# A zeroing that waits for the first normalised tiles, and a weight load that changes queue

## The chip, the cores and the metric

The kernel runs on one core of a Trainium2 chip. The core has five engines with instruction queues of their own: TensorE (PE in the profile; its weight loads are listed as PEld), VectorE (DVE), ScalarE (ACT), GpSimd (POOL) and SyncE (SP), which here only issues DMA transfers. Any of the engines can issue transfers; the DMA engines behind them are shared. The metric is the device time of one execution in microseconds, as the median of several runs. The time before is 667.74 us, the median of three runs (665.72, 667.74 and 669.32).

## The reference

The input x has 2048 rows of 512. It is normalised by rows, and the result xn feeds two branches whose product is added to x:

```python
xn = _layernorm(x, axis=-1)
s = _A_ref(xn, A_wq, A_wk, A_wv, A_wo)   # attention: 32 heads of 16 for q, one shared k and v
g = _silu(_B_ref(xn, B_w1, B_w2))        # silu(xn @ w1) @ w2, F = 1792
return x + s * g
# in _A_ref:
scores = jnp.einsum("bhqd,bkd->bhqk", q, k) * (Dh ** -0.5)
p = _softmax(scores, axis=-1)
o = jnp.einsum("bhqk,bkd->bhqd", p, v)
```

With 32 heads, 2048 queries and 2048 keys there are 134 million exponentials, and the head dimension is only 16.

## The kernel before, in words

**Tiling.** The 2048 queries are cut into four chunks of 512 and the 32 heads into eight groups of four, which gives 32 groups (gi). For each group the keys go by in 16 tiles of 128. One score block has 128 keys by 512 queries of one head. TensorE computes the score blocks of four heads in four row strips of its array (`score`, L622). Keys are kept in two layouts, kTa and kTb (`kT_sb[0]` and `kT_sb[1]`). Even groups read kTa, odd ones kTb, whose rows are copied from kTa by DMA inside SBUF (`move_K`, L510: four transfers of 16 KB for each chunk of keys, on SyncE's queue).

**Exponentials.** Most blocks go to ScalarE, two at a time (`exp_A`, L653, 128 x 1024). The rest go to VectorE, which builds the bit pattern of an approximate exponential as int16 (`exp_D`, L691); GpSimd adds constants to it for two more terms (`shift`, L716). The product of the weights with v (L776) gathers in the bank psO.

**Masked q.** The tile `qm_sb` has four rows of blocks, one for each head of a group, zero everywhere except in the 32 partitions of its head. With it, a score block can also be computed by the whole array in column form (`col_fill`, which goes through the helper `columns`, L401). `mask_q` (L1324) fills the four rows by four DMA transfers of 32 KB from `qT_sb`, on SyncE's queue. Before that the tile has to be zeroed once: that is the memset at L389, on GpSimd. Each later refill of a row waits until the matmuls that read the row are done.

**The start.** Four tiles of x arrive; VectorE and ScalarE make their statistics, ScalarE takes the square root (L443), and VectorE normalises the four tiles (`normalise`, L450). TensorE transposes them (`first_T`, L477), ScalarE and VectorE copy the transposes out of PSUM in turn (L482, L484), then come the first keys and queries, and with them the first exponential. TensorE is kept busy until then by 13 warm-up matmuls on zeros (L408). The other twelve tiles of x are normalised beside the first exponentials; this is called the front in the code. When the last chunk of keys is there, `front_evac` calls `move_K` and then `late_loads`, which asks for wo (L395, on SyncE's queue) and w2 (L396, on ScalarE's queue). w1 was asked for earlier (L392, SyncE). The hidden layer (`h` jobs, w1) and its second product (`z` jobs, w2) fill TensorE between score blocks, through L401.

**The order.** A planner in Python (`Sched` and the loop at the end) lays out all instructions when the kernel is built. It models the time of every engine, t, and appends each operation to its engine's list. On the chip, each engine works its list off in order. An operation that reads or writes what another engine or a transfer still uses gets a semaphore wait, and the instructions behind it on the same engine wait too. The planner's times decide the order only; they do not delay anything on the chip.

Of the kernel before, what the change touches and what calls it, by code (L numbers as in the profile page):

```python
# [13 lines left out]
P = 128  # L14
# [21 lines left out]
class Sched:  # L36
# [107 lines left out]
    def op(self, eng, fn, reads=(), writes=(), lane=None, cost=None):  # L144
        who = lane or eng
        if lane:
            self.lanes[lane] = eng
        n = self.done.get(who, 0)
        self.done[who] = n + 1
        deps = self.deps(eng, reads, writes)  # L150
        self.at[(who, n)] = self.model(eng, lane, cost, max([self.at[d] for d in deps.items()], default=0.0))
        clk = self.clock.setdefault(eng, {})
        waits = []
        cand = [(f, m) for f, m in deps.items() if clk.get(f, -1) < m]
        for f, m in cand:
            implied = False
            for f2, m2 in cand:
                if (f2, m2) != (f, m) and self.snap[(f2, m2)].get(f, -1) >= m:
                    implied = True
            if not implied:  # L160
                waits.append((f, m))
        for f, m in cand:
            for g, k in self.snap[(f, m)].items():
                if clk.get(g, -1) < k:
                    clk[g] = k
            if clk.get(f, -1) < m:
                clk[f] = m
        for f, m in waits:
            self.flagged.setdefault(f, set()).add(m)
        self.snap[(who, n)] = dict(clk)  # L170
        self.queues.setdefault(eng, []).append((fn, waits, who, n))
        for r in reads:
            self.readers.setdefault(r, {})[who] = n
        for w in writes:
            self.last_w[w] = (who, n)
            self.readers[w] = {}
        return who, n
# [36 lines left out]
def bass_recurrent_scan__grouped_kv_mqa__dense_activation_silu__prompt_kernel(  # L214
# [69 lines left out]
        P=(0.25, 3.0, 0.65, 10, 1.2, 2.0, 0, 12, 0.2, 3, 3, 0.0, 0.35, 0.43, 0, 0.33, 0, 1, 9, 9),  # L284
# [10 lines left out]
        a=(0.3, 3.0, 0.65, 10, 1.2, 2.0, -4, 24, 0.2, 3, 3, 0.04, 9, 0.43, 0, 0.33, 0, 0, 9, 9),  # L295
# [5 lines left out]
    with ExitStack() as es:  # L301
        def sb(name, shape, dt=BF16):
            return es.enter_context(nc.sbuf_tensor(name, shape, dt))
# [11 lines left out]
        w2_sb = sb("w2_sb", [P, NFT, D])  # L315
# [11 lines left out]
        qm_sb = sb("qm_sb", [P, 4, NQ])  # L327
# [21 lines left out]
        op = K.op  # L349
# [5 lines left out]
           reads=["ident"], writes=["ident"])  # L355
# [19 lines left out]
        for j in range(NPH + 1):  # L375
# [10 lines left out]
        wkp4 = wkp_sb[:, :, :].rearrange("p c (r e) -> p c r e", e=32)  # L386
        op("gp", lambda e: e.tensor_copy(wkp4[:, :, :, 0:DH], wkn_sb[:, :, :].unsqueeze(2).to_broadcast([P, NDC, 4, DH])),
           reads=["wkn", "wkp"], writes=["wkp"])
        op("gp", lambda e: e.memset(qm_sb[:], 0.0), writes=[("qm", i) for i in range(4)], cost=1.8)  # L389

        def load_w1():
            op("sp", lambda e: e.dma_start(w1_sb[:], B_w1.rearrange("(dc p) f -> p dc f", p=P)), writes=["w1"], lane="lw1", cost=7.0)  # L392

        def late_loads():
            op("sp", lambda e: e.dma_start(wop_sb[:], A_wo.rearrange("(t p) n -> p t n", p=P)), writes=["wop"], lane="lwo", cost=4.0)  # L395
            op("a", lambda e: e.dma_start(w2_sb[:], B_w2.rearrange("(ft p) n -> p ft n", p=P)), writes=["w2"], lane="lw2", cost=9.0)  # L396

        def columns(e, bank, lhsT, rhs, start, stop):

# [13 lines left out]
        def tiles(c):  # L413
            return range(4 * c, 4 * c + 4)
# [34 lines left out]
        def normalise(t, eng):  # L449
            op(eng, lambda e: e.tensor_scalar(xn_sb[:, t % 8, :], x_sb[:, t, :], mv_sb[:, t, 0:1], rstd_sb[:, t:t + 1],  # L450
                                              op0=ALU.subtract, op1=ALU.mult),
               reads=[("x", t), ("mv", t), ("rstd", t // 4)], writes=[("xn", t % 8)], cost=0.41)
# [18 lines left out]
        def first_T(t, bank, key, eng):  # L471

            ps = bank.bitcast(BF16)[:, 0:NQ]

            def f(e):
                for dc in range(NDC):
                    r = e.transpose(ps[:, dc * P:(dc + 1) * P], xn_sb[:, t, dc * P:(dc + 1) * P], ident[:, :])  # L477
                return r
            op("pe", f, reads=[("xn", t), "ident"], writes=[key], cost=("full", [None] * 4, P))
            dst, src = xnT_sb[:, :, t * P:(t + 1) * P], ps.rearrange("p (dc q) -> p dc q", dc=NDC)  # L480
            if eng == "a":
                op("a", lambda e: e.activation(dst, src, ACT.Copy), reads=[key], writes=[("xnT", 0, t)])  # L482
            else:
                op("v", lambda e: e.tensor_copy(dst, src), reads=[key], writes=[("xnT", 0, t)])  # L484
# [71 lines left out]
        rstd_sqrt(0)  # L556
        for t in tiles(0):
            normalise(t, "v")
        first_T(0, psD[:, 0:NQ], "D", EV[0])
        first_T(1, psD[:, NQ:2 * NQ], "D1", EV[1])  # L560
        first_T(2, psO[:, :], "O", EV[2])
# [377 lines left out]
        def group_A():  # L939
            if ast["tile"] is not None:  # L940
                return ast["tile"][0]
            return next((gi for gi in range(NGRP) if left[gi] or halves.get(gi)), NGRP)
# [207 lines left out]
        qm = dict(of=-1)  # L1150
# [59 lines left out]
        def meets(t):  # L1210

            x = needed() + SLIP - t
            return 0 if x >= 0 else 1 + int(-x / 0.9175)

        def v_cand():

            tv = K.free["v"] - 0.084
            cand = [(max(tv, K.ready("v", tk["reads"], tk["writes"])), tk) for tk in tasks if all(n in tok for n in tk["need"])]
            d, blks = 1e9, dst["fifo"][:1]
            if blks and may_D(blks):  # L1220
                blk = blks[0]
                d = max(tv, K.ready("v", [blk["bank"]], [ph_key(0, slot_of[blk["idx"]], blk["pos"])]))
                two = dst["fifo"][:2]
                if len(two) == 2 and (two[0]["bank"], two[1]["bank"]) == ("D", "D1") and two[0]["idx"] == two[1]["idx"] and may_D(two):
                    d2 = max(tv, K.ready("v", ["D", "D1"], [ph_key(0, slot_of[b["idx"]], b["pos"]) for b in two]))
                    if d2 <= d + 0.1 and (JOINT or meets(d + 0.735) >= meets(d2 + 1.27)):
                        d, blks = d2, two
            return cand, d, blks

        def advance_v(t):  # L1230

            while True:
                cand, d, blks = v_cand()
                first = min([x for x, _ in cand] + [d])
                if first >= t:
                    return
                now = [(x, tk) for x, tk in cand if x <= first + 0.01]
                now.sort(key=lambda p: (p[1]["kind"] != "gn1", p[1]["kind"] in ("gn2", "gn3", "gn4", "add"), RANK.get(p[1]["kind"], 1), p[1].get("born", 0.0)))
                pick = now[0][1] if now else None
                if pick is not None and pick["kind"] == "st":  # L1240
                    soon = [(x, tk) for x, tk in cand if tk["kind"] in ("T", "K", "nm", "ag") and x < first + 0.35]
                    pick = min(soon, key=lambda p: p[0])[1] if soon else pick
                if pick is not None and d < first + pick["cost"] and first - pick.setdefault("born", first) < AGES.get(pick["kind"], AGE):
                    cost = 1.221 if len(blks) == 2 else 0.687
                    if meets(d + cost + 0.05) < meets(first + pick["cost"] + cost):
                        pick = None
                if pick is not None:
                    tasks.remove(pick)
                    pick["run"](pick)
                elif d < t:  # L1250
                    dst["fifo"] = dst["fifo"][len(blks):]
                    exp_D(blks)
                else:
                    return
# [151 lines left out]

        K.act_end = max(K.act_end, FIRST)
        K.free["a"] = max(K.free["a"], FIRST - 0.3)
        now, gp_end = 0.0, False
        while state["g"] < NGRP or front or jobs or jst["open"] or tasks:  # L1410
            (SLIP, ROUND, KEEP, HOLD, AGES["gn1"], AGE, F_BEHIND, ENDQ, PVWAIT, LEAD, AHEAD, MARGIN, XGAIN, AIM, TWIN,
             TGATE, FRESH, JOINT, CGAIN, CLEFT) = \
# [1 line left out]
            t = max(now, min(K.pe_next("col"), K.pe_next("full")))  # L1414
            if t > 2000.0:
                raise ValueError(f"the order does not end {state} {jobs[:3]} {jst} {tasks} {dst} {ast}")
            advance_v(t + 0.05)
            more = group_A() < NGRP
            if tanh_ready(K.act_end - TGATE if more else t):
                emit_tanh()  # L1420
            if not more and not gp_end and not dst["open"] and not dst["fifo"]:
                op("gp", lambda e: e.tensor_tensor(mhalf_sb[:, :], mhalf_sb[:, :], mhalf_sb[:, :], ALU.add),
                   reads=["mhalf"], writes=["mhalf"])
                gp_end = True
# [5 lines left out]
            if more:  # L1430
# [4 lines left out]
                if TWIN and K.pe_mode == "row" and not front and release() <= K.pe_next("row") + 0.12:  # L1435
                    slots, t = 0, K.pe_next("row")
# [41 lines left out]
            if TWIN and more and not blocked and did and not front and tanh_ready(K.act_end - TWIN):  # L1478
                emit_tanh()
                now = 0.0  # L1480
                continue
            if more and not blocked:
# [6 lines left out]
                now = 0.0  # L1489
            elif not did:  # L1490
                if dst["open"]:
                    fill_D(t, [0, 1, 2, 3])
                now = t + 0.05
            else:
                now = 0.0
# [38 lines left out]
        for k in (0, 1):  # L1534
# [13 lines left out]
           writes=[("out", t0), ("out", t0 + 1)], lane="st01a")  # L1548
# [40 lines left out]
```

## Time and profile before

| what | value |
|---|---|
| median of three runs | 667.74 us (665.72 to 669.32) |
| the profiled execution's own time | 666.98 us |
| its span, first to last instruction | 665.2 us |
| TensorE busy | 652.6 us (98%) |
| ScalarE busy | 652.6 us (98%), of which L653 630.9 us |
| VectorE busy | 597.5 us (90%) |
| GpSimd busy | 384.2 us (58%) |
| w2's load: KB, us from issue to landing | 1792, 9.5 |
| w1's load | 1792, 8.5 |

In the timeline a line has its start, its length, the engine, the line of the kernel, the operation, the tile written and the tile read, the shape and a count; in brackets stands how long the engine was idle before it and what ended that idle time. "xN" is N like instructions in a row, told as one. In a table of stages, each engine has its busy time and the number of instructions; then come the clock granted to TensorE, the mean busy share of the DMA engines, and GB/s. A busy TensorE is not a TensorE at full speed, since matmuls overlap and their ends are modelled.

### The profile page before, as it was taken

Reading aid. Unit: us, or ns where it says so; the run is one execution under the profiler, and the core shown is the slowest. Engines: PE = TensorE matmul, PEld = TensorE weight load, DVE = VectorE, ACT = ScalarE, POOL = GpSimd, SP = SyncE. Lnnn points to the kernel's source line nnn. Section 1 sums busy time; section 2 is a strip of 40 time slices with the busy share of each in tenths; the row PEclk is TensorE's granted clock in tenths of the full one; section 3 lists DMA queues with packets and bytes.
Section 4 is the critical chain, followed back from the end, with each engine's and each line's share of the span. In section 5 each row is a group of like instructions: output and inputs, shape, how many; then the busy total and the mean of one; then the engine's idle time right before and its main releaser. Section 6 shows DMA issues by size and latency. Waiting matters only on the chain.

```text
span 665.2 us, 18816 instructions
## 1 busy us (share of the span) xinstructions
PE 652.6 (98%) x8199; PEld 184.7 (28%) x8201; DVE 597.5 (90%) x1023; ACT 652.6 (98%) x754; POOL 384.2 (58%) x388
## 2 busy tenths in 40 slices
PE   8989999999999999999999999999999999999996
PEld 4422222222222222222222222222222222222221
DVE  7979899989888988989989889999999898898995
ACT  7979999999999999999999999999999999999997
POOL 4247455657655657565666656566665566675563
PEclk9979999999999999999999999999999999999999
DMA  5540000000000000100000000010000000000110
GB/s 168 160 153 2 1 8 6 2 9 2 6 1 10 2 25 18 39 4 2 9 2 6 6 3 2 8 33 26 25 4 5 1 8 16 1 2 2 33 34 33
DMA packets 15394, 14.61 MB, mean 22 GB/s; under 512 B 3536, under 2 KB 14800, under 8 KB 15312
## 3 DMA queue, kind: packets, MB, share of 16 engines
q1 hardware_dynamic: 12944, 11.05, 5.6%
q10 hardware_dynamic: 2368, 2.36, 1.2%
q8 instruction: 64, 1.05, 0.7%
q14 instruction: 18, 0.15, 0.1%
HBM read 8.95 MB, written 2.10 MB: 17 GB/s over the span
## 4 chain that ended last, share of the span: by engine, by line
ACT 77%; PE 17%; DVE 3%; DMA 1%; SPq 1%; issue 0%
ACT pa_sb L653 72%; PE psO L776 6%; PE psA L622 6%; ACT t_sb L1092 5%; PE psF L401 4%; DMA qm_sb<-qT_sb 1%; DVE stats_sb L417 1%; PE psD L461 0%; DMA x_sb<-in_A_x_dram 0%; DVE xn_sb L450 0%; SPq L510 0%; PE psD L492 0%; DVE kTa_sb L504 0%; PE psA L669 0%; DVE ph_sb L691 0%
## 5 line engine op out<-in xcount | busy, mean ns | idle before, releaser
L653 ACT ACTIVATE pa_sb<-psA 128x1024 bf16<-128x1024 f32 x662 | 630.9, 1220 | 5.0 <-PE psD L622 2.8
L716 POOL INT64_ADD ph_sb<-ph_sb x290 | 300.0, 1047 | 200.6 <-DVE ph_sb L691 200.4
L691 DVE TENSOR_SCALAR ph_sb<-psD 128x512 int16<-128x512 f32 (+1 forms) x520 | 348.0, 689 | 36.6 <-PE psD L622 31.7
L776 PE MATMUL psO<-ph_sb,vaug_sb 128*32 128x512 bf16 x1740 | 215.1, 384 | 0.0
L776 PE MATMUL psO<-pa_sb,vaug_sb 128*32 128x512 bf16 (+1 forms) x1332 | 201.3, 382 | 0.6 <-DVE onb_sb L888 0.6
L622 PE MATMUL psA<-qT_sb,kTa_sb 32*128 32x512 bf16 x684 | 132.7, 384 | 2.4 <-ACT pa_sb L653 1.2
L622 PE MATMUL psA<-qT_sb,kTb_sb 32*128 32x512 bf16 x632 | 123.1, 387 | 1.1 <-ACT pa_sb L653 0.6
L622 PE MATMUL psD<-qT_sb,kTb_sb 32*128 32x512 bf16 x325 | 114.7, 386 | 0.1
L716 POOL INT64_ADD x_sb<-x_sb x72 | 74.2, 1043 | 47.5 <-DVE x_sb L691 47.5
L691 DVE TENSOR_SCALAR x_sb<-psD 128x512 int16<-128x512 f32 x132 | 89.2, 684 | 12.6 <-PE psD L622 10.0
L622 PE MATMUL psD<-qT_sb,kTa_sb 32*128 32x512 bf16 x287 | 99.9, 384 | 0.0
L776 PE MATMUL psO<-x_sb,vaug_sb 128*32 128x512 bf16 x432 | 77.6, 383 | 0.0
L622 PEld LDWEIGHTS psA<-qT_sb,kTa_sb 32*128 32x128 bf16 x684 | 32.2, 91 | 143.1 <-ACT pa_sb L653 129.6
L401 PE MATMUL psF<-xnT_sb,w_sb 128*32 128x512 bf16 x896 | 69.8, 384 | 0.0
L401 PE MATMUL psF<-w_sb,u_sb 128*32 128x512 bf16 x896 | 69.5, 384 | 0.0
L622 PEld LDWEIGHTS psA<-qT_sb,kTb_sb 32*128 32x128 bf16 x632 | 29.8, 91 | 136.6 <-ACT pa_sb L653 121.4
L776 PEld LDWEIGHTS psO<-ph_sb,vaug_sb 128*32 128x32 bf16 x1740 | 53.2, 95 | 47.1 <-issue 30.4
L776 PEld LDWEIGHTS psO<-pa_sb,vaug_sb 128*32 128x32 bf16 x1332 | 48.9, 95 | 39.8 <-issue 29.4
L1092 ACT ACTIVATE t_sb<-psF 128x512 bf16<-128x512 f32 x72 | 57.8, 803 | 0.0
L1124 DVE SCALAR_TENSOR_TENSOR u_sb<-t_sb,psF 128x512 bf16<-128x512 bf16 x56 | 38.0, 679 | 4.9 <-ACT t_sb L1092 4.5
L691 DVE TENSOR_SCALAR ph_sb<-psF 128x512 int16<-128x512 f32 x52 | 35.4, 681 | 0.0
L622 PEld LDWEIGHTS psD<-qT_sb,kTb_sb 32*128 32x128 bf16 x325 | 27.5, 91 | 2.0 <-DVE ph_sb L691 1.1
(133 smaller groups left out, 368.1 us busy)
## 6 DMA issues: line engine op xcount, KB each, us to landing
x_sb<-in_A_x_dram SPq DMA_DIRECT2D x18, 128.0 KB, 2.2
qm_sb<-qT_sb SPq DMA_DIRECT2D x64, 32.0 KB, 1.8
w_sb<-in_B_w_dram SPq DMA_DIRECT2D x1, 1792.0 KB, 8.5
w_sb<-in_B_w_dram ACTq DMA_DIRECT2D x1, 1792.0 KB, 9.5
out_dram<-ob_sb SPq DMA_DIRECT2D x14, 128.0 KB, 1.7
x_sb<-in_A_x_dram SPq DMA_DIRECT2D x3, 512.0 KB, 6.6
wop_sb<-in_A_wo_dram SPq DMA_DIRECT2D x1, 512.0 KB, 7.9
wq_sb<-in_A_wq_dram SPq DMA_DIRECT2D x1, 384.0 KB, 6.1
```

The costliest lines, as they stand in the source:

```text
L401: r = e.matmul(bank[32 * i:32 * i + 32, :], lhsT=lhsT[:, 32 * i:32 * i + 32], rhs=rhs, start=start, stop=stop, tile_position=(0, 32 * i), ...
L417: op("v", lambda e: e.bn_stats(stats_sb[:, t, :], x_sb[:, t, :]), reads=[("x", t)], writes=[("st", t)], cost=0.687)
L622: return e.matmul(ap, lhsT=kT_sb[g % 2][32 * i:32 * i + 32, kt * P:(kt + 1) * P], rhs=qT_sb[32 * i:32 * i + 32, c % 2, g // 2, :], start=T ...
L653: d = op("a", lambda e: e.activation(pa_sb[:, sl, :], psA[k][:, :], ACT.Exp, scale=ESCALE), reads=["A%d" % k], writes=[("pa", sl)], cost=2 ...
L691: d = op("v", lambda e: e.tensor_scalar(ph_ap(0, sl, 512 * pos, 512 * pos + m), src, float(PH_ONE + PH_BIAS), 0.0, op0=ALU.add, op1=ALU.ma ...
L716: d = op("gp", lambda e, j=j: e.int64_add(ph_ap(j, sl, 0, 4 * NQ).bitcast(I64), ph_ap(0, sl, 0, 4 * NQ).bitcast(I64), PH_SHIFT[j] * 0x0001 ...
L776: r = e.matmul(psO[32 * i:32 * i + 32, cs], lhsT=vaug_sb[:, p["v"], p["kt"], :], rhs=p["ap"], start=s0, stop=s1, tile_position=(0, 32 * i) ...
L1092: op("a", lambda e: e.activation(t_sb[:, n % 2, :], bank_ap(b), ACT.Tanh, scale=0.5 if jb[0] == "h" else 0.25), reads=[b], writes=[("t", n ...
L1124: op("v", lambda e: e.scalar_tensor_tensor(out=dst, in0=t_sb[:, n % 2, :], scalar=1.0, in1=src, op0=ALU.add, op1=ALU.mult), reads=tk["read ...
```

## The change

Two things are edited. The memset that zeroes `qm_sb` is issued later in GpSimd's list's making, and it now reads ("xn", 3), the fourth normalised tile, so GpSimd waits for that tile before it zeroes. The load of w2 is taken out of `late_loads` and ScalarE's list. It becomes a function of its own, `load_w2`, on SyncE's list, which the planner's loop calls once, when its modelled time t first passes 60.

```diff
-        op("gp", lambda e: e.memset(qm_sb[:], 0.0), writes=[("qm", i) for i in range(4)], cost=1.8)
...
         def late_loads():
             op("sp", lambda e: e.dma_start(wop_sb[:], A_wo.rearrange("(t p) n -> p t n", p=P)), writes=["wop"], lane="lwo", cost=4.0)
-            op("a", lambda e: e.dma_start(w2_sb[:], B_w2.rearrange("(ft p) n -> p ft n", p=P)), writes=["w2"], lane="lw2", cost=9.0)
+
+        def load_w2():
+            op("sp", lambda e: e.dma_start(w2_sb[:], B_w2.rearrange("(ft p) n -> p ft n", p=P)), writes=["w2"], lane="lw2", cost=9.0)
...
         for t in tiles(0):
             normalise(t, "v")
+        op("gp", lambda e: e.memset(qm_sb[:], 0.0), reads=[("xn", 3)], writes=[("qm", i) for i in range(4)], cost=1.8)
...
-        now, gp_end = 0.0, False
+        now, gp_end, w2_asked = 0.0, False, False
...
             advance_v(t + 0.05)
+            if not w2_asked and t > 60:
+                load_w2()
+                w2_asked = True
```

## The prediction

> **What bounds the kernel now.** I read the page first: busy shares, the slices and the chain that ended last.
>
> ```profile
> span 665.2 us, 18816 instructions
> PE 652.6 (98%) x8199; PEld 184.7 (28%) x8201; DVE 597.5 (90%) x1023; ACT 652.6 (98%) x754; POOL 384.2 (58%) x388
> ACT 77%; PE 17%; DVE 3%; DMA 1%; SPq 1%; issue 0%
> ...
> L653 ACT ACTIVATE pa_sb<-psA 128x1024 bf16<-128x1024 f32 x662 | 630.9, 1220 | 5.0 <-PE psD L622 2.8
> ```
>
> ScalarE's exponentials (L653) are the bound. They run back to back from about 11 to 640 us, and of their 5.0 us of idle time the list of waits puts all in a few places. So only two things can shorten the run: an earlier first exponential, or less idle time between them. The timeline of ScalarE shows where that idle time is:
>
> ```profile
> 10.80 20.28 ACT L653 ACTIVATE pa_sb<-psA 128x1024 bf16<-128x1024 f32 x22 [0.59 <-PE psA L622]
> 30.89 0.39 ACTq L396 DMA_DIRECT2D w_sb<-in_B_w_dram  x1
> 30.92 8.41 ACT L653 ACTIVATE pa_sb<-psA 128x1024 bf16<-128x1024 f32 x9
> 40.39 1.02 ACT L653 ACTIVATE pa_sb<-psA 128x1024 bf16<-128x1024 f32 x1 [1.07 <-PE psD L622]
> 43.00 1.02 ACT L653 ACTIVATE pa_sb<-psA 128x1024 bf16<-128x1024 f32 x1 [1.58 <-PE psA L622]
> 44.94 1.02 ACT L653 ACTIVATE pa_sb<-psA 128x1024 bf16<-128x1024 f32 x1 [0.92 <-PE psD L622]
> 46.46 1.02 ACT L653 ACTIVATE pa_sb<-psA 128x1024 bf16<-128x1024 f32 x1 [0.50 <-PE psD L622]
> 47.82 7.44 ACT L653 ACTIVATE pa_sb<-psA 128x1024 bf16<-128x1024 f32 x8 [0.34 <-PE psD L622]
> ```
>
> Between 39.3 and 47.8 us ScalarE loses 1.07 + 1.58 + 0.92 + 0.50 + 0.34 = 4.41 us to late score matmuls. What made those late stands in TensorE's timeline and in the stages of that stretch (columns of the latter: PE, PEld, DVE, ACT, POOL busy, granted clock, DMA share, GB/s):
>
> ```profile
> 39.31 0.09 PEld L622 LDWEIGHTS psF<-qT_sb,kTb_sb 32*128 32x128 bf16 x1 [1.10 <-DMA kTb_sb<-kTa_sb]
> ...
> 41.80 0.11 PEld L401 LDWEIGHTS psD<-qm_sb,kTb_sb 128*32 128x32 bf16 x4 [1.42 <-DMA qm_sb<-qT_sb]
> ```
>
> ```profile
> 36.00:38.00 2.00, 2.00 (x24) 0.50 (x21) 1.83 (x3) 2.00 (x3) 0.70 (x2) 1.00 1.10 368
> 40.00:42.00 2.00, 0.88 (x15) 0.27 (x11) 1.74 (x3) 1.02 (x1) 0.00 (x0) 0.67 0.30 72
> 42.00:44.00 2.00, 2.00 (x18) 0.40 (x14) 0.85 (x2) 1.00 (x1) 0.74 (x1) 0.50 0.13 33
> 44.00:46.00 2.00, 2.00 (x18) 0.35 (x14) 1.03 (x2) 1.04 (x2) 1.31 (x2) 0.50 0.13 33
> ```
>
> The first two losses are TensorE waiting for copies inside SBUF (second key layout kTb, masked q). The last three are its clock, granted at 0.50 until past 46 us, with 512-column matmuls at 0.60 instead of 0.39 us. The DMA engines were full until 40 us, with w2's 1.8 MB, issued at 30.89 and 9.5 us in flight, as the largest part.
>
> The start is read on VectorE and GpSimd:
>
> ```profile
> 5.19 1.80 POOL L389 MEMSET qm_sb<- 128x2048 bf16 x1
> ...
> 6.04 1.10 DVE L450 TENSOR_SCALAR xn_sb<-x_sb,mv_sb,rstd_sb 128x512 bf16<-128x512 bf16 x1
> ...
> L450 DVE TENSOR_SCALAR xn_sb<-x_sb,mv_sb,rstd_sb x16: 395/407/1096, 6.0 to 27.6; 128x512 bf16<-128x512 bf16 x16
> ```
>
> The first normalise takes 1.10 us, the median of sixteen 0.41, and it ends 0.1 us after the memset does.
>
> **The change part by part.** Built, both programs have the same instructions in the same order on TensorE and VectorE. ScalarE loses one DMA issue, SyncE gains it between the eighth and ninth mask copy, and GpSimd's memset keeps its place and gains a wait. So nothing is reshuffled and the sum can be made by places.
>
> *Memset behind the fourth normalise.* The first normalise falls from 1.096 to 0.407, 0.69 us less, so all four end near 7.42 instead of 8.10. Two things may eat part of this: the warm-up matmuls, whose last starts at 6.27 and holds TensorE until about 6.6 (0.51 us less the usual overlap), and ScalarE's table load and its dummy exponential, which end at 7.31. With transposes every 0.32 us from 6.6, the second is done near 7.35 and ScalarE copies it out at 7.37 instead of 7.95: 0.58 less. VectorE's next input, the 512 KB of x issued at 2.65, lands 5.4 us later, at 8.05 by its issue's start or 8.56 by its end; the statistics that need it began at 8.69 and could begin at 8.1. In the second case they gain 0.1 only, and the key copy behind them (11.35) costs about 0.3 of the gain. Bounds 0.3 and 0.69; I take 0.5, nearer the earlier landing.
>
> The memset itself now runs from about 7.45 to 9.25. Behind it on GpSimd is only the inverse root at 11.5. Beside it lie two VectorE copies out of PSUM (L484, 0.41 each) and the statistics (0.68). Statistics beside the earlier memset of kTb (3.10 to 4.90) took 2.01 us for three, 0.67 each, so they are free. No row shows a bf16 copy out of PSUM beside a memset. Lower bound nothing, by L691, out of PSUM beside GpSimd all through (mean 0.689, and 0.68 with GpSimd idle); upper bound a block to the memset's end, as for the first normalise: the second copy then ends at 9.65 instead of 8.77, 0.9 us later than before. I take nothing, since L691 shares the PSUM source. On this the Trainium skill ("SBUF — State Buffer", Who interferes with whom; "VectorE: DVE Perf Modes", Mode 2×_2P) says that GpSimd and VectorE share one port pair under an exclusive lock, taken by VectorE's two-port modes, and that these need source and destination in SBUF. By that rule the copies are free as well; the 1.096 us row agrees with the lock, and no run here yet shows the copies.
>
> *w2 off ScalarE's queue.* The issue took 0.39 us, but exponentials come every 0.917 us (22 in 20.28) and the next began at 30.92, on that beat: 0 gained.
>
> *w2 out of 31 to 40 us.* Four kTb copies, issued from 31.0 to 32.8, took 5.9 us (median) to land beside w2. The same copies took 2.3 and 2.0 us at 12 and 26 us with no large load, and 4.5 beside w1. Mask rows took 7.5, 6.7, 6.2, 5.7 us beside w2, 1.8 later. Without w2, the kTb copies land by about 35.5; their first late reader stood at 37.7 and both kTb waits go. The masks are issued from 34.1 behind wop's 512 KB; at the 368 GB/s seen at 36 us that is 1.4 us, so rows land at about 37 to 38.2. The column matmul that waited until 41.80 then comes at 41.80 − 1.42 − 1.10 − 0.39 (the first kTb wait) = 38.9, the row it reads (the second, issued at 35.04) having landed near 37. TensorE's pauses vanish, and with them the half clock. Everything is 0.5 earlier in both, which changes no margin. The recovery is at most 4.41. What is late next is VectorE: from 36.51 to 48.72 it has eleven 512-column operations at 0.61 spacing and 0.6 of small ones, 7.3 us, in the 12.2 − 4.4 = 7.8 us left. That fits, with little to spare. I take 4.2, bounds 3.4 and 4.41.
>
> The Trainium skill ("TensorE: Matmul & The Clock Gate", Part 1) states that the clock halves after an idle window of about 3.4 us and returns after as long a busy one. The rows agree roughly: TensorE was busy 1.98 us of 38 to 42 and at half rate for some 6 us. Its use here is against me: a shorter pause could still halve the clock.
>
> *w2 at its new place.* "t > 60" is the planner's time, not the chip's; on the chip w2 goes out once the eighth mask copy has. The sixth must wait for the column matmul just named (42.47 behind 41.80 in the trace), so w2 cannot run before it. It goes at about 40 to 41 and lands about 9.5 us later, near 50. It is first read at 144.9. SyncE's issue may take 1.34 us (w1's row); behind it stands one mask row that waited until 46.29 for q and is not read before 97. No kTb copy is left. ScalarE kept 0.92 us per exponential beside w2 (8.41 for nine). Cost 0.
>
> Sum: 0.5 + 4.2 = 4.7 us. The profiled execution took 666.98 us (span 665.2 and 1.8 around it), 0.76 below the median 667.74; the runs are 665.72 to 669.32. If the spread is the DMA race itself, the new kernel sheds it and 662.3 holds; if not, 663.0. I take 662.6, on a base of 667.3.
>
> **Rivals.**
> 1. *Copies blocked by the memset.* For it: the 1.10 us row. Against: L691. The front loses 0.9 instead of gaining 0.5: 667.3 − 4.2 + 0.9 = 664.0. Chance 0.07.
> 2. *Another DMA takes w2's place*: wop and the four x reloads (1 MB together) still delay the mask row, and the clock still drops. Then 1.58 + 0.92 + 0.50 + 0.34 stay and 1.07 + 0.5 are gained: 665.7. Against: 1 MB is 2.9 us at 368 GB/s and half of it lands before the masks are issued. Chance 0.10.
> 3. *The pauses are not w2's*: only the front gains, 666.8. Against: landing times of 2 and 1.8 us wherever no large load flies. Chance 0.04.
> 4. *Slower: TensorE's instruction fetch behind w2.* Instruction packets of 16 KB were fetched at 14–16, 24–26, 40–42, 50–55 us: roughly every 10 us, except 15 while w2 was in flight. With w2 at 41 to 50, a fetch may land late when TensorE needs it. A delay like the mask rows' (7.5 − 1.8 = 5.7) with the clock's drop (0.92 + 0.50 + 0.34 = 1.8) costs 7.5, less 4.7: 670.1. It decides from 4.7 us of stall. Against: no fetch beside w1 or w2 is named in any wait. Chance 0.04.
>
> **How the numbers follow.** My forecast has 0.75, its own range 661.9 to 664.0 (the profiled time less 5.1, the median less 3.7). The whole range reaches 0.9 lower, for half of what the runs spread below their median, and up to 665.5, which takes in rival 1 and the near side of 2: 661.0 to 665.5, with about 0.18 outside. About 0.5% (3.3 us) is what can be told from no change: 664.4 is the line. Faster: 0.75 nearly whole, half of rival 1, a little of 2: 0.79. Slower: most of rival 4: 0.03. Same: 0.18.
>
> **What would show it.** Right: the first normalise at 0.41 us and the first exponential near 10.3; kTb copies landing in 2 to 3 us and no DMA wait at the column matmul; clock 1.00 from 36 to 50; the exponentials without gaps there; w2 issued by SyncE near 41. Wrong: a copy of L484 longer than 0.41, a mask row still landing in over 4 us, or a gap in TensorE between 41 and 50 that names no semaphore.

## The result, and the profile after

The changed kernel takes 661.88 us (median of six runs, 661.39 to 662.37), against 666.96 us for the kernel before (now six runs, 665.72 to 669.32). The ratio is 0.9921, with a 95% interval of 0.9903 to 0.9939: faster by 0.8%, and inside the range that was forecast. The profiled execution took 661.39 us, the lowest of the six, with a span of 659.6, which is 5.6 less than the span before.

The timeline of ScalarE, of the changed kernel, answers to the one with five pauses:

```profile
10.13 39.53 ACT L655 ACTIVATE pa_sb<-psA 128x1024 bf16<-128x1024 f32 x43 [0.59 <-PE psA L624]
49.50 0.65 ACT L1094 ACTIVATE t_sb<-psF 128x512 bf16<-128x512 f32 x1
```

The first exponential comes at 10.13 instead of 10.80, and 43 of them follow without a pause. The first tanh (L1092 before, L1094 now) stood at 55.07 and stands at 49.50. So 5.57 of the 5.6 us between the two profiles are won by then, and nothing is given back later.

In the stages of the same stretch (PE, PEld, DVE, ACT, POOL busy, granted clock, DMA share, GB/s) the clock stays at 1.00 and the DMA engines are nearly empty (0.06) when the masks are read, at 38.3; w2 now flies from 41 to 48.6:

```profile
38.00:40.00 2.00, 2.00 (x28) 0.58 (x26) 2.00 (x5) 2.00 (x3) 1.31 (x2) 1.00 0.06 16
40.00:42.00 2.00, 2.00 (x28) 0.47 (x26) 2.00 (x6) 2.00 (x3) 1.31 (x2) 1.00 0.19 49
42.00:44.00 2.00, 2.00 (x28) 0.54 (x25) 2.00 (x4) 2.00 (x3) 0.74 (x1) 1.00 0.92 234
44.00:46.00 2.00, 2.00 (x28) 0.61 (x31) 2.00 (x5) 2.00 (x4) 1.69 (x2) 1.00 1.07 376
```

The DMA view of 30 to 52 us gives the landing times (last column, us):

```profile
w_sb<-in_B_w_dram SPq DMA_DIRECT2D x1, 1792.0 KB, 7.8
wop_sb<-in_A_wo_dram SPq DMA_DIRECT2D x1, 512.0 KB, 4.4
qm_sb<-qT_sb SPq DMA_DIRECT2D x9, 32.0 KB, 3.8
kTb_sb<-kTa_sb SPq DMA_DIRECT2D x4, 16.0 KB, 1.8
```

The last four kTb copies land in 1.8 us, where they took 5.9. The mask rows still take about 4 us behind wo (4.1, 4.0, 4.2 and 3.8 for the first four).

At the start, the timeline of VectorE and GpSimd:

```profile
6.05 1.38 DVE L451 TENSOR_SCALAR xn_sb<-x_sb,mv_sb,rstd_sb 128x512 bf16<-128x512 bf16 x4
...
7.35 0.42 DVE L485 COPY xnT_sb<-psD 128x512 bf16<-128x512 bf16 x1
...
7.50 1.80 POOL L560 MEMSET qm_sb<- 128x2048 bf16 x1 [1.72 <-DVE xn_sb L451]
7.69 0.41 DVE L485 COPY xnT_sb<-psO 128x512 bf16<-128x512 bf16 x1
```

Four normalises take 1.38 us, not 2.06. The second copy out of PSUM runs inside the memset and takes its usual 0.41.

### The profile page after: what moved, and what is told of

Its sections match the earlier page's. It is cut to its first block, busy times and chain, and to the rows that moved or that the text cites. A ratio compares the mean times of both kernels' runs of the same rounds, so it can differ in the third digit from the quotient of the medians.

```text
span 659.6 us, 18816 instructions
## 1 busy us (share of the span) xinstructions
PE 649.5 (98%) x8199; PEld 185.3 (28%) x8201; DVE 596.3 (90%) x1023; ACT 652.0 (99%) x754; POOL 384.2 (58%) x388
## 4 chain that ended last, share of the span: by engine, by line
ACT 83%; PE 16%; DVE 1%; issue 0%
ACT pa_sb L655 78%; PE psO L778 6%; ACT t_sb L1094 5%; PE psA L624 5%; PE psF L402 3%; PE psF L409 1%; PE psA L671 0%; DVE wq_sb L1527 0%; DVE otr_sb L888 0%; DVE xn_sb L894 0%; PE psD L624 0%; PE psD L478 0%; DVE wq_sb L1522 0%; PE psO L493 0%; DVE onb_sb L890 0%
## 5 line engine op out<-in xcount | busy, mean ns | idle before, releaser
L1094 ACT ACTIVATE t_sb<-psF 128x512 bf16<-128x512 f32 x72 | 57.9, 805 | 0.0
L1126 DVE SCALAR_TENSOR_TENSOR u_sb<-t_sb,psF 128x512 bf16<-128x512 bf16 x56 | 38.1, 680 | 4.7 <-ACT t_sb L1094 4.3
```

What stands on the lines that cost most here:

```text
L1094: op("a", lambda e: e.activation(t_sb[:, n % 2, :], bank_ap(b), ACT.Tanh, scale=0.5 if jb[0] == "h" else 0.25), reads=[b], writes=[("t", n ...
L1126: op("v", lambda e: e.scalar_tensor_tensor(out=dst, in0=t_sb[:, n % 2, :], scalar=1.0, in1=src, op0=ALU.add, op1=ALU.mult), reads=tk["read ...
```

## The experiments

Each was run beside the kernel before on the same chip, in three batches on three chips: the first four below, the next four, and the last three, which were run once each. The kernel before took 666.98, 666.95 and, in one run, 667.45 us there. The changed kernel was not run again in these batches, so its 661.88 us is from another batch than theirs. Apart from the edits shown, the instructions of all engines keep their order in the traces.

**Each edit alone.** The first kernel moves the memset only, the second w2 only.

```diff
 # memset only, against the kernel before
-        op("gp", lambda e: e.memset(qm_sb[:], 0.0), writes=[("qm", i) for i in range(4)], cost=1.8)
...
             normalise(t, "v")
+        op("gp", lambda e: e.memset(qm_sb[:], 0.0), reads=[("xn", 3)], writes=[("qm", i) for i in range(4)], cost=1.8)
```

> Only the memset waits for the fourth normalised tile; w2 stays on ScalarE's queue at its old place. My theory (the two edits act in separate places and add): the first exponential comes 0.67 us earlier as in the changed kernel, the pauses of 39 to 48 us stay, so about 0.7 us below the kernel before. Rival (the front's gain is swallowed, since with the same late transfers the column matmul waits for the mask row until the same moment): 0 to 0.2 us below, with the pauses longer by what the front gained.

Measured: 666.00 us (663.85 to 667.23) against 666.98 (664.30 to 670.58); ratio 0.9978, interval 0.9961 to 0.9995. The profiled run took 663.85, and ScalarE's timeline has only two of the five pauses:

```profile
10.17 20.29 ACT L653 ACTIVATE pa_sb<-psA 128x1024 bf16<-128x1024 f32 x22 [0.59 <-PE psA L622]
...
39.41 1.02 ACT L653 ACTIVATE pa_sb<-psA 128x1024 bf16<-128x1024 f32 x1 [0.71 <-PE psD L622]
41.78 10.35 ACT L653 ACTIVATE pa_sb<-psA 128x1024 bf16<-128x1024 f32 x11 [1.34 <-PE psA L622]
```

The front gains 0.6 us as expected, and it is not swallowed. But this profile is the fastest of the twelve executions, and in it only two of the pauses stay, where the expectation had all of them. In this execution TensorE's weight loads waited for transfers nearly as long as in the first profile of the kernel before (0.89, 0.25 and 1.61 us, 2.75 together, against 0.39, 1.10 and 1.42, 2.91 together). Yet the granted clock stayed at 1.00, and the three later pauses are missing. So the pauses for transfers and the pauses after them are two things. How often the later ones come shows in the mean granted clock that is on record for each execution. The 23 executions of the kernel before in this batch fall into steps: 664.3 and 665.3 us at 0.999, 665.8 to 666.8 at 0.996 and 0.997, 666.8 to 668.2 at 0.994 and 0.995, and 668.9 to 670.6 at 0.992. Most of the spread of the kernel before goes with its time at half clock.

```diff
 # w2 only, against the changed kernel
+        op("gp", lambda e: e.memset(qm_sb[:], 0.0), writes=[("qm", i) for i in range(4)], cost=1.8)
         def load_w1():
...
             normalise(t, "v")
-        op("gp", lambda e: e.memset(qm_sb[:], 0.0), reads=[("xn", 3)], writes=[("qm", i) for i in range(4)], cost=1.8)
```

> Only w2 is moved; the memset stays ahead of the normalised tiles. My theory: all pauses between 39 and 48 us go, 4.41 us of idle time and 0.1 us more for each of the five, since exponentials that follow on each other overlap by 0.1 us: 4.9 us below the kernel before, the first exponential still at 10.8 us. Rival (the two edits need each other): clearly less than 4.4 us.

Measured: 662.28 us (662.05 to 663.28), ratio 0.9923, interval 0.9900 to 0.9945. First exponential at 10.79, then 43 without a pause, first tanh at 50.17: 4.90 ahead of the kernel before, as expected (the figure was worked out from the changed kernel's profile, which was known by then). By the medians it is 4.70 less. The two edits act in separate places and add.

**The queue or the time.** One kernel asks for w2 late, but on ScalarE's queue. Another asks for it on SyncE's queue, but at the old place behind wo.

```diff
 # late on ScalarE's queue, against the changed kernel
         def load_w2():
-            op("sp", lambda e: e.dma_start(w2_sb[:], ...), writes=["w2"], lane="lw2", cost=9.0)
+            op("a", lambda e: e.dma_start(w2_sb[:], ...), writes=["w2"], lane="lw2", cost=9.0)
```

> Both edits, but w2 is asked for late on ScalarE's queue (between exponentials near 58 us) and not on SyncE's. My theory (the time of the transfer matters, not the queue): same as the changed kernel within 0.4 us, 5.1 us below the kernel before; the issue of 0.39 us hides under a running exponential. Rival (ScalarE's queue was part of the cost): 0.4 us or more slower than the changed kernel, with a gap between exponentials at the issue.

Measured: 661.45 us (661.41 to 661.91), ratio 0.9908, interval 0.9888 to 0.9928. The issue at 59.85 takes 0.39 us under a running exponential, and no pause follows. ScalarE's queue was no part of the cost.

```diff
 # early on SyncE's queue, against the changed kernel
         def late_loads():
             op("sp", lambda e: e.dma_start(wop_sb[:], ...), writes=["wop"], lane="lwo", cost=4.0)
+            op("sp", lambda e: e.dma_start(w2_sb[:], ...), writes=["w2"], lane="lw2", cost=9.0)
...
-            if not w2_asked and t > 60:
-                load_w2()
-                w2_asked = True
```

> Both edits, but w2 goes out on SyncE's queue at the old place: right behind wo, ahead of the first mask rows, behind the last kTb copies. My theory: kTb copies land in 2 to 2.5 us, but the mask rows stand behind 2.3 MB and land 6 to 8 us after their issue, at about 41 to 42; the column matmul waits 3 us or more and the clock drops, so nearly all of the gain but the front's is lost: 0 to 2 us below the kernel before. Rival (the queue change alone is the gain): 5 us below, as the changed kernel.

Measured: 668.93 us (668.50 to 669.69), ratio 1.0021, interval 1.0007 to 1.0036: slower than the kernel before, although the front's gain is in it. The expectation missed the time: it gave 0 to 2 us below the kernel before, and it is 1.95 us above. The wait and the drop of the clock came as the theory had them, but larger. TensorE's waits, ScalarE's timeline and two stages show it:

```profile
PE psD L401 <- DMA qm_sb<-qT_sb: 5.2, 1, 5.2
```

```profile
10.18 29.80 ACT L654 ACTIVATE pa_sb<-psA 128x1024 bf16<-128x1024 f32 x32 [0.59 <-PE psA L623]
45.54 1.02 ACT L654 ACTIVATE pa_sb<-psA 128x1024 bf16<-128x1024 f32 x1 [5.56 <-PE psA L623]
47.48 1.02 ACT L654 ACTIVATE pa_sb<-psA 128x1024 bf16<-128x1024 f32 x1 [0.92 <-PE psD L623]
```

```profile
42.00:44.00 2.00, 0.00 (x0) 0.00 (x0) 0.00 (x0) 0.00 (x0) 0.00 (x0) 0.50 0.19 51
44.00:46.00 2.00, 1.66 (x14) 0.52 (x18) 0.85 (x2) 0.46 (x1) 0.20 (x1) 0.50 0.06 16
```

The kTb copies, issued ahead of w2, land in 1.8 us and TensorE no longer waits for them. The mask rows, issued behind w2 on the same queue, land 8.6 us after their issue (median of the first two) instead of 5.7 to 7.5. From 42 to 44 us no engine is busy, and TensorE resumes at 44.34, at half clock. What the transfer is put ahead of decides the cost.

**Half of w2 early.** If the cost went with the bytes in flight, half of w2 at the old place would cost half.

```diff
 # against the changed kernel
         def late_loads():
             ...
+            op("a", lambda e: e.dma_start(w2_sb[:, 0:7, :], ...), writes=["w2"], lane="lw2a", cost=5.0)
...
         def load_w2():
-            op("sp", lambda e: e.dma_start(w2_sb[:], ...), writes=["w2"], lane="lw2", cost=9.0)
+            op("sp", lambda e: e.dma_start(w2_sb[:, 7:14, :], ...), writes=["w2"], lane="lw2b", cost=5.0)
```

> Both edits, but w2 is loaded in two halves of 0.9 MB: the first at the old place on ScalarE's queue, the second late on SyncE's. My theory (the wait is as long as the transfers ahead): with 0.9 MB less in flight at 30 us the DMA engines are full until about 37 and not 40; kTb copies land in about 3 to 4 us, still in time for 37, and the mask rows near 38.5 to 39.5 against a reader at 38.5. So a wait of 0 to 1 us and no drop of the clock: 0 to 1 us above the changed kernel, a threshold and no proportion. Rival (cost in proportion to the bytes in flight): half of the 4.9 us comes back, 2.4 us above the changed kernel.

Measured: 661.52 us (661.12 to 662.46), ratio 0.9923, interval 0.9907 to 0.9939. The kTb copies take 4.7 us, more than the 3 to 4 expected, and the mask rows about 4, and yet TensorE waits for neither and the exponentials have no pause. The last kTb copy lands at about 36.1 and is read at 36.7; the second mask row lands at about 37.7 and is read at 38.1. At half of w2 the cost is none, not half: it is a threshold, and a transfer costs nothing as long as it lands ahead of its reader.

**w2 three times over.** This is the rival by which a load beside the steady state would hold up TensorE's instructions.

```diff
 # against the changed kernel
         def load_w2():
-            op("sp", lambda e: e.dma_start(w2_sb[:], ...), writes=["w2"], lane="lw2", cost=9.0)
+            for n in range(3):
+                op("sp", lambda e: e.dma_start(w2_sb[:], ...), writes=["w2"], lane=f"lw2{n}", cost=9.0)
```

> As the changed kernel, but w2 is loaded three times over, one after the other, from 41 to about 66 us, so that TensorE's instruction packets (one every 10 us) must come in beside it. My theory: no engine waits for anything in that stretch, as the changed kernel within 0.3 us. Rival (instruction fetch suffers beside a large load): a gap in TensorE that names no semaphore, 1 us or more above the changed kernel, with the clock's drop up to 7 us.

Measured: 661.50 us (661.28 to 661.92), ratio 0.9920, interval 0.9905 to 0.9936. The three loads follow on each other from 41 to about 64 us. TensorE waits for no transfer and the exponentials have no pause; from the first tanh to the second it is 9.53 us, against 9.54 in the changed kernel. Beside 5.4 MB of loads the steady state loses nothing.

**wo late too.** In the changed kernel the second mask row is issued at 33.98 and lands 4.0 us later, at about 38.0; the weights that read it are loaded at 38.33.

```diff
 # against the changed kernel
         def late_loads():
-            op("sp", lambda e: e.dma_start(wop_sb[:], ...), writes=["wop"], lane="lwo", cost=4.0)
+            pass
...
         def load_w2():
+            op("sp", lambda e: e.dma_start(wop_sb[:], ...), writes=["wop"], lane="lwo", cost=4.0)
             op("sp", lambda e: e.dma_start(w2_sb[:], ...), writes=["w2"], lane="lw2", cost=9.0)
```

> As the changed kernel, but wo's 512 KB too are asked for late, right ahead of w2. In the changed kernel the second mask row landed 4.0 us after its issue at 33.98, only 0.3 to 0.6 us ahead of its reader at 38.3. My theory: mask rows land in 1.8 us, the margin grows to over 2 us, and the time stays that of the changed kernel within 0.3 us, with no wider spread. Rival (in the unprofiled runs the row is often too late): 0.3 to 1 us below the changed kernel and a smaller spread.

Measured: 661.46 us (661.27 to 661.54), ratio 0.9919, interval 0.9903 to 0.9934. Mask rows land in 1.8 to 2.4 us. The time is that of the half load and of the triple load in the same batch (661.52 and 661.50), whose rows come behind wo; whether the narrower spread of four runs (0.3 us against 1.0 of six) is an effect is not settled by so few.

**Work in the waits.** The kernel before, with matmuls on zeros near the places where TensorE waited, so that the transfers stay late and only idle time of TensorE goes.

```diff
 # against the kernel before; the planner's times are put back after it
+        def ghost(n, key):
+            ...
+            op("pe", f, reads=["zero"], writes=[key], cost=("full", [None] * n, NQ))
...
+                if bank == "F" and o["tile"][0] == 1 and "ghost1" not in tok:   # ahead of the block that waits for kTb
+                    tok.add("ghost1")
+                    ghost(4, "F")
...
+            if "ghost2" not in tok:                                             # ahead of the column matmul
+                tok.add("ghost2")
+                ghost(5, "F")
```

> The kernel before, w2 and memset at their old places, with nine matmuls on zeros added to TensorE's list: four ahead of the score block that waits for kTb, five ahead of the column matmul that waits for the mask row. They fill the waits and shorten none. My theory (the last three pauses are the clock's): granted clock 1.00 from 38 to 50, the pauses of 0.92, 0.50 and 0.34 us go with 0.1 of overlap each, the first two stay: about 2 us below the kernel before, with a smaller spread, since runs without a drop of the clock no longer differ from runs with one. Rival (the later pauses are a backlog behind the late row, not the clock): no faster than the kernel before, or slower by up to 1 us for the added matmuls.

Measured: 665.71 us (665.28 to 668.23) against 666.95 (665.27 to 669.53); ratio 0.9987, interval 0.9974 to 0.9999. ScalarE's timeline of the profiled run:

```profile
12.95 20.28 ACT L653 ACTIVATE pa_sb<-psA 128x1024 bf16<-128x1024 f32 x22 [0.59 <-PE psA L622]
...
43.41 1.02 ACT L653 ACTIVATE pa_sb<-psA 128x1024 bf16<-128x1024 f32 x1 [1.94 <-PE psD L622]
45.58 10.35 ACT L653 ACTIVATE pa_sb<-psA 128x1024 bf16<-128x1024 f32 x11 [1.14 <-PE psA L622]
```

The first four matmuls came behind the wait for kTb (0.87 us, still idle), the other five filled the wait for the mask row. The clock stays at 1.00 from 36 to 50 us, and the three later pauses are gone although the row is still late. Over the executions it is the same: nine of the twelve have a mean granted clock of 0.999 or more (665.3 to 666.2 us), against one of the seventeen of the kernel before (665.27). The later pauses belong to the clock, not to a backlog. The gain is about 1.2 and not 2 us. The first two pauses grew from 2.65 to 3.08, partly by the added matmuls (the score block at 42.34 had to follow them). The start of the profiled run is 2.15 us late, which the next experiments explain.

**Where the zeroing stands.** Two kernels put part or all of the memset elsewhere ahead of the normalises, and one is the kernel before once more.

```diff
 # half: two rows at the old place, two behind the fourth tile; against the changed kernel
+        op("gp", lambda e: e.memset(qm_sb[:, 0:2, :], 0.0), writes=[("qm", i) for i in range(2)], cost=0.95)
...
-        op("gp", lambda e: e.memset(qm_sb[:], 0.0), reads=[("xn", 3)], writes=[("qm", i) for i in range(4)], cost=1.8)
+        op("gp", lambda e: e.memset(qm_sb[:, 2:4, :], 0.0), reads=[("xn", 3)], writes=[("qm", i) for i in range(2, 4)], cost=0.95)
 # first: the whole memset ahead of wk's copy; against the changed kernel
+        op("gp", lambda e: e.memset(qm_sb[:], 0.0), writes=[("qm", i) for i in range(4)], cost=1.8)
         wkp4 = wkp_sb[:, :, :].rearrange("p c (r e) -> p c r e", e=32)
...
-        op("gp", lambda e: e.memset(qm_sb[:], 0.0), reads=[("xn", 3)], writes=[("qm", i) for i in range(4)], cost=1.8)
```

> As the changed kernel, but two of the four rows of masked q are zeroed at the old place (about 0.9 us from 5.2, or later where wk lands late) and the other two behind the fourth normalised tile. My theory (GpSimd holds VectorE off for the rest of its memset, whatever is left of it): the first normalise ends about 0.1 us after that half memset if the half still runs at 6.05, else it takes 0.41 us; with the half ending near 6.1 the first exponential comes near 10.15 to 10.25. Rival (a running memset costs a normalise 0.69 us, however short it is): first normalise at 1.1 us, first exponential at 10.8.

> As the changed kernel, but the whole memset stands ahead of wk's copy on GpSimd, right behind the memset of kTb, so it runs from 4.9 to 6.7 without waiting for wk's landing. My theory: the first normalise is held until 6.7 to 6.8, 0.3 us less than in the kernel before and 0.35 more than in the changed one; first exponential near 10.45. Rival (the copy of wk's keys, not the memset, held VectorE): first normalise at 0.41 us, first exponential near 10.1.

One run each: 661.47 us for the half and 661.84 for the memset ahead of wk's copy, beside 667.45 for the kernel before. The timelines of GpSimd and VectorE, of the half and then of the early whole:

```profile
5.20 0.95 POOL L389 MEMSET qm_sb<- 128x1024 bf16 x1
...
5.94 0.73 DVE L452 TENSOR_SCALAR xn_sb<-x_sb,mv_sb,rstd_sb 128x512 bf16<-128x512 bf16 x2
```

```profile
4.84 1.80 POOL L386 MEMSET qm_sb<- 128x2048 bf16 x1
...
6.05 0.73 DVE L452 TENSOR_SCALAR xn_sb<-x_sb,mv_sb,rstd_sb 128x512 bf16<-128x512 bf16 x1
```

A memset that ends at 6.15 costs a normalise begun at 5.94 nothing (two take 0.73, the usual pace). One that ends at 6.64 holds the normalise to 6.78. First exponentials: 10.14 and 10.52, as my theory had them. Both rivals fall. Where the memset ran on, the normalise ended 0.14 us behind it, in the kernel before 0.15 (6.99 and 7.14). That only the last part of its 0.41 us is held off fits these times; no run shows it in another way.

> The kernel before, unedited, for a second profile of it, since its runs spread from 664.3 to 670.6 us and one profile shows one of them. My theory (two things vary: whether the pauses near 40 us let the clock drop, worth about 2 us, and when wk lands, which sets when the memset meets the normalises, worth up to 2 us): this profile shows either a clock of 1.00 from 42 to 48 us with a time near 665, or a clock of 0.50 there with a time near 667; and a memset that starts where wk's copy ends. Rival (the spread is elsewhere): the same pauses and the same start as in the first profile, with a time more than 1 us off 667.

Measured: 669.68 us. Its timelines of GpSimd, VectorE, TensorE and ScalarE, and a stage:

```profile
5.49 0.40 POOL L387 COPY wkp_sb<-wkn_sb 128x256 bf16<-128x256 bf16 x1 [0.59 <-DMA wkn_sb<-in_A_wk_dram]
5.84 1.80 POOL L389 MEMSET qm_sb<- 128x2048 bf16 x1
```

```profile
6.34 1.45 DVE L450 TENSOR_SCALAR xn_sb<-x_sb,mv_sb,rstd_sb 128x512 bf16<-128x512 bf16 x1
```

```profile
7.85 0.88 PE L477 MATMUL psD<-ident,xn_sb 128*128 128x128 bf16 x8 [1.90 <-DVE xn_sb L450]
```

```profile
12.76 20.28 ACT L653 ACTIVATE pa_sb<-psA 128x1024 bf16<-128x1024 f32 x22 [0.63 <-PE psA L622]
```

```profile
8.00:10.00 2.00, 2.00 (x22) 1.88 (x21) 1.90 (x6) 0.98 (x2) 0.00 (x0) 0.56 1.04 347
```

Here wk's copy had to wait for wk and began at 5.49 instead of 4.85. The memset stands behind that copy and so ran from 5.84 to 7.64. The first normalise began 0.30 us later than in the first profile, took 1.45 us and ended at 7.79. TensorE stood idle for 1.90 us between its warm-up and the first transposes, and its clock was 0.50 from about 8.2 to 11.7. The first exponential came at 12.76, 1.96 later than in the first profile; 0.65 of it was there when the first normalise ended, the rest came after, in the stretch at half clock. Near 40 us the pauses were 1.19, 2.76, 0.92 and 0.32. So the start varies as my theory had it; both causes fell the bad way at once, which the expectation had not named (it gave 665 or 667). The profiled run with matmuls in the waits had the same kind of start: wk's copy at 6.11, a memset to 8.39, the second normalise held to 8.55. In the changed kernel's profile wk's copy was late too, at 5.38, and nothing was held.

## Why the prediction was right, point by point

- *The memset.* The first normalise fell to its usual length and the first exponential came 0.67 earlier; I took 0.5, with 0.69 as the bound. The 512 KB of x was there in time (statistics at 8.02), so the bound from the issue's start was the true one. What a late wk adds was not in the forecast. The profile I reasoned from shows a mild case of the hold; in two of the three other profiles with the whole memset behind wk's copy the first exponential came another 2 us later, by a longer hold and a dropped clock. How often that happens is not shown.
- *The copies beside the memset* were free: 0.416 and 0.414 us. Rival 1 falls. The Trainium skill ("SBUF — State Buffer", Who interferes with whom) says that a VectorE instruction with at most one input in SBUF, outside the two-port modes, does not contend with GpSimd. These copies agree with it.
- *w2 off ScalarE's queue*: nothing, as said; asking late on ScalarE's queue gives 661.45. Rival 3 falls as well: with only w2 moved all five pauses go.
- *w2 out of 31 to 40 us.* The recovery was 4.90 us, not 4.2, and over the upper bound of 4.41. The step that was off is the bound. ScalarE's idle time counts from an exponential's end, but exponentials that follow on each other overlap: each is 1.02 long, and they come 0.917 apart. Each of the five pauses therefore cost about 0.1 us more than its idle time, and 4.41 became 4.90. The forecast's own range, 661.9 to 664.0, was worked out from these bounds, and 661.88 lies just below it; only the room of 0.9 us left for the spread of the runs takes it in. VectorE did not come late next: it was busy all of 38 to 48 us, and ScalarE never waited.
- *Where masks stand.* I had the second row landing near 37, about 2 us after its issue, and its reader at 38.9, both less the 0.5 us of the front. The reader came at 38.3, as that gives. The row was issued at 33.98 and took 4.0 us behind wo's 512 KB, so it landed at 38.0. The margin was 0.3 us, not 1.9. My own sign of being wrong, a mask row landing in over 4 us, was met by two rows (4.1 and 4.2), and still nothing waited. That no wait came was thus nearer to luck than I said, and rival 2 nearer than its chance of 0.10, though half of w2 in flight did not trigger it.
- *The later pauses are the clock's.* Right: they vanish where TensorE works through the wait, and where the clock happens not to drop. The clock also has a part of the second pause, which I gave to the transfer alone: from the first masked matmul to the exponential it is 1.20 us in the first profile (41.80 to 43.00), and 0.76 in the two where the clock stayed at 1.00 (41.02 to 41.78, 44.82 to 45.58).
- *Slower by instruction fetch.* Not seen, even beside three loads.
- *The base.* The sum was 4.7 us against 5.57 between the two profiles and 5.08 between the medians. The time of 662.6 was 0.72 above 661.88: 0.38 by the sum, 0.34 by the base, 667.3 against a median that six runs put at 666.96. That the new kernel sheds the spread was right: 1.0 us over six runs, where 23 runs of the kernel before on one chip spread over 6.3.

## What to carry to other kernels

Ask for a large load behind the small transfers that someone will wait for soon, and look at what stands ahead of those; in this kernel another queue did not protect them. A late transfer costs nothing as long as it lands ahead of its reader. A pause of TensorE is to be priced with the half clock that can follow it, and a pause of an engine whose instructions overlap with the lost overlap. A GpSimd memset that waits, directly or behind another instruction, on a landing time should be tied to a point where VectorE's work from SBUF to SBUF that others wait for is done.

## What was not expected of the hardware

- A normalise out of SBUF that began beside a running GpSimd memset ended 0.14 to 0.16 us behind the memset in four profiles (6.64 to 6.78, 6.99 to 7.14, 7.64 to 7.79, 8.39 to 8.55), not a whole 0.41 us behind it, and one that overlapped a memset by 0.2 us lost nothing.
- The clock drops for whole stretches. In the first profile of the kernel before it was 0.50 from 40.7 to 47.5 us, 6.8 us in all: a mean clock of 0.67 in the stage from 40 to 42 puts the drop there, and 0.63 in this one the return:

```profile
46.00:48.00 2.00, 2.00 (x22) 0.37 (x19) 1.43 (x4) 1.21 (x2) 0.00 (x0) 0.63 0.06 16
```

  The clock records of the other traces give 6.83 us again (second profile, from 42.38), 10.24 us (w2 early on SyncE's queue, from 40.31) and 3.41 us twice (the two late starts): one, two or three times 3.41. What brings a drop stays open. Idle time alone does not: near 40 us, waits of 2.91 us in all dropped the clock in one profile and waits of 2.75 did not in another; at the start an idle stretch of 1.90 us dropped it and one of 1.33 us (the memset ahead of wk's copy) did not. The Trainium skill ("TensorE: Matmul & The Clock Gate", Part 1) puts the drop after at least one idle window of about 3.4 us, and says that the window runs freely. The length of the stretches agrees with such a window. The idle window does not: in the 3.41 us ahead of the five drops TensorE was busy for 1.51 to 2.51 us. The prediction's "agree roughly" was too kind to the Trainium skill there.
